# A cross network in Strassen form: the last unit's stores on other queues and in a new order, and two kinds of transposes at set times

## The chip, the cores and the metric

The kernel runs on one core of a Trainium2 chip. A core has TensorE (PE, matrix products), VectorE (DVE), ScalarE (ACT), GpSimd (POOL) and SyncE (SP), each with its own in-order queue of instructions, and DMA queues that SP, ACT and POOL fill and that share 16 DMA engines. The metric is the time of one execution on the device in microseconds; lower is better. Three executions of the kernel before took 2214.38, 2215.24 and 2218.46 us: the median is 2215.24 us.

## The reference

```python
x = x0                       # 16384 x 1024, bfloat16
for l in range(6):
    proj = x @ ws[l] + bs[l]     # ws[l]: 1024 x 1024
    x = x0 * proj + x
return x
```

Six layers, each a full matrix product of 16384 x 1024 by 1024 x 1024, followed by a product with the input x0 and the residual.

## The kernel before

**Work and tiles.** The 16384 rows are cut into 16 pairs of 1024 rows. A *unit* is one layer of one pair, so there are 96 units; two pairs form a group and take turns through the six layers (unit 2k is a layer of the even pair, unit 2k+1 the same layer of the odd pair), and the groups follow each other. Twelve units make a group; seven times in the program one group ends and the next begins. x is held transposed, as four quadrants of 512 features by 512 rows (`00`, `01`, `10`, `11`: feature half, row half).

**Products.** A unit does the 2x2 block product in Strassen-Winograd form with seven products P1 to P7 of 512 x 512 x 512 in place of eight. Each is four groups (`P1.0` to `P1.3`, by column block) of four matmuls 128x128 by 512 columns. Most units do three or four of the seven products with a second level of the same scheme (`5p1` to `5p7` and so on, groups of four matmuls with 256 columns). The sums of x's quadrants (T1 to T4) and the combination of the products (Q, U, V, W) are made on DVE; ACT takes results out of PSUM. The sums of weights are made once, in the first group, stored to DRAM (`Lc`) and reloaded for each later group into a ring of 12 buffers (`wp`).

**Order.** The program is written as named operations with engine, estimated duration and what they read and write. `schedule` (L69) makes from these a list by time, engine by engine: among those ready, the one with the earliest due time goes first; TensorE's order is given by hand in lists (`PE_FIRST` to `PE_LAST`, L17 to L44), one per kind of unit. `at=` gives an operation a time before which it isn't placed. These times only set the order in which instructions stand on each queue; on the chip an instruction runs when its queue reaches it and its semaphores are there. `plan_loads` (L146) puts the weight loads among them, and `pump` (L307) sends them on SP.

**SP's queue.** It carries the weight loads (L315), the loads of x0, which transpose from DRAM (`load`, L415; the DMA is L418), the transposes of finished results into row order (`tro`, L743; the DMA is L744) and their stores (`sto`, L751; L753), and most of the end's work. At a group boundary all four kinds meet: the next group's weights, the next odd pair's x0 (L436 to L438, loaded while unit l = 0 of the even pair runs), and the outputs of the finished even pair. There the lower two quadrants of x0 (`10` and `11`) are placed after `P4.0` of the unit two before:

```python
                load(pr, q, ARRIVE["next"] if u == 1 else 0.0, after=[f"ld11.{pr - 1}@{u - 4}"] + ([f"P4.0@{u - 2}"] if q[0] else []) if grp > 0 else ())
```

and the even pair's output transposes have no set time (L746).

**The last unit** (number 95, `last`) has only one level of products. Its four output quadrants leave by two ways. Q and the two halves U0 and U1 are put into x0's buffer by DVE, transposed by SP (`trQ`, `trU0`, `trU1`, L681) and stored by POOL's software queue (`stQ`, `stU0`, `stU1`, L684). V and W are transposed by TensorE (`tV.m`, `xW.m`, `tW.m`, L693, four of 128 columns each), copied out of PSUM by ACT and DVE (L703, L705) and stored in halves of 256 KB (`stVa`, `stVb`, `stWa` on SP, `stWb` on ACT, L712). While this goes on, the results of the other pair (number 14) leave by `tro` and `sto`.

Of the kernel before, what the change touches and what calls it, by code (L numbers as in the profile page):

```python
# [38 lines left out]
3p6 P7.0 4p2 3p3 4p6 3p7 P7.1 4p7 4p3 3p4 P7.3 P7.2 4p4  # L39
""".split()  # L40
PE_LAST = """
P1.0 P1.2 P1.3 P1.1 P2.0 P2.2 P2.1 P2.3 P6.0 P5.2 P5.1 P6.1 P5.0 P5.3 P3.1 P6.2 P3.0 P6.3 P3.2 P3.3 P7.0 P7.1 P7.3
P7.2 P4.0 P4.3 P4.2 tV.0 tV.1 xW.3 P4.1 xW.0 xW.2 tV.2 tV.3 xW.1 tW.0 tW.2 tW.3 tW.1
""".split()  # L44
ARRIVE = {"rows0": 4.9, "w0.1": 6.4, "rows1": 8.9, "rows2": 11.3, "w0.2": 11.9, "h0": 14.3, "h1": 15.5, "q": 17.5, "next": 21.0, "raw1": 40.0}

# [2 lines left out]
RING = 12  # L49
LOAD, BURST, LEAD, GRACE = 1.45, 2.9, 13, 4  # L50
STORED, SPARE = 12.0, 14.0
UNIT, LET = 22.68, 54.0
LOAD_ORDER = "1 5 2i 5i 4 2 3i 6 4i 3 7".split()
TURN = [
# [3 lines left out]
]  # L58


class Op:
# [130 lines left out]
def kernel(  # L192
# [7 lines left out]
    nc = tc.nc  # L200
# [4 lines left out]
    KH = KD // 2  # L205
# [5 lines left out]
    NGROUP = NPAIR // 2  # L211
# [136 lines left out]
    for u, (pr, l) in enumerate(units):  # L348
# [86 lines left out]

        if l == 0 and lane == 1:  # L436
            for q in QD:
                load(pr, q, ARRIVE["next"] if u == 1 else 0.0, after=[f"ld11.{pr - 1}@{u - 4}"] + ([f"P4.0@{u - 2}"] if q[0] else []) if grp > 0 else ())  # L438

        if grp == 0 and lane == 0:  # L440
            raw = lambda w, gl=gl: wt[(gl, w)]
# [188 lines left out]
        if not last:  # L630
            if not one:
                ttop("Q1", Q[:], Q[:], P1s[:], ADD, allm("Q") + allm("P1s"), allm("Q"))
            if not one:
                ttop("Ub", U[:], U[:], C3[:], ADD, allm("U") + allm("3c"), allm("U"))
            if "4" in inn:
                ttop("Wa", W[:], W[:], V[:], ADD, allm("W") + allm("V"), allm("W"))
            ttop("Ua", U[:], U[:], P5s[:], ADD, allm("U") + allm("5c"), allm("U"))
            ttop("Va", V[:], V[:], P5s[:], ADD, allm("V") + allm("5c"), allm("V"))
            for nm, C, q in (("Q", Q, (0, 0)), ("U", U, (0, 1)), ("V", V, (1, 1)), ("W", W, (1, 0))):
                if l == 0:  # L640
                    ttop(nm + "m", xblk(xst, *q), C[:], x0j(*q), MULT, allm(nm) + [X0[q]], [XO[q]] + ISW)
                    continue
                ttop(nm + "m", C[:], C[:], x0j(*q), MULT, allm(nm) + [X0[q]], allm(nm))
                if nm in DMA_RES.get(l, ""):
                    def acc(C=C, q=q, xst=xst):
                        nc.gpsimd.dma_start(xblk(xst, *q), C[:], accum_op=ADD)  # L646
                    op(f"{nm}x@{u}", "POOL", 1.0, ACCUM[(grp > 0) + (grp > 0 and l == L - 2 and lane)], acc, allm(nm) + [XO[q], "xbar"], [XO[q]])
                else:
                    ttop(nm + "x", xblk(xst, *q), C[:], xblk(xst, *q), ADD, allm(nm) + [XO[q]], [XO[q]])
        else:  # L650
            F0, F1 = (pr - 1) % 3, (pr - 2) % 3
            quad = lambda t: flat(t).rearrange("r (e n j k p) -> r e n j k p", e=2, n=2, j=KH, p=P)
            xfin, xo = quad(x0Ts[F0]), quad(xsts[F1])
            halves = lambda t: flat(t)[:, KH * NB:2 * KH * NB].rearrange("r (h j k p) -> r h j k p", h=2, j=KH, p=P)
            xfU, xoU = halves(x0Ts[F0]), halves(xsts[F1])
            XF = [f"x0.{F0}.{a}{b}" for a, b in QD]
            XT = [f"xs.{F1}.{a}{b}" for a, b in QD]
            r0 = pr * PR
            END = NU * 22.8
            half = lambda s, h: [f"{s}.{2 * h}", f"{s}.{2 * h + 1}"]  # L660
            ttop("Qm", Q[:], Q[:], x0j(0, 0), MULT, allm("Q") + [X0[0, 0]], allm("Q"))
            ttop("Qa", xfin[:, 0, 0], Q[:], xsj(0, 0), ADD,
                 allm("Q") + [XI[0, 0]] + XF, ["xfQ0", "xfQ1"])
            for h in range(2):
                sl = slice(h * KQ, (h + 1) * KQ)
                for nm, C, q in (("U", U, (0, 1)), ("V", V, (1, 1))):
                    ms = half(nm, h)
                    ttop(f"{nm}a{h}", C[:, :, sl], C[:, :, sl], P5s[:, :, sl], ADD, ms + half("5c", h), ms, n=1024)
                    ttop(f"{nm}m{h}", C[:, :, sl], C[:, :, sl], x0j(*q)[:, :, sl], MULT, ms + [X0[q]], ms, n=1024)
                ttop(f"Vx{h}", V[:, :, sl], V[:, :, sl], xsj(1, 1)[:, :, sl], ADD, half("V", h) + [XI[1, 1]], half("V", h), n=1024)  # L670
                ttop(f"Ux{h}", xfU[:, h], U[:, :, sl], xsj(0, 1)[:, :, sl], ADD, half("U", h) + [XI[0, 1]] + XF, [f"xfU{h}"], n=1024)
            for m in range(KH - 1):
                ttop(f"Wm{m}", mcol(W, m), mcol(W, m), mcol(x0j(1, 0), m), MULT, [f"W.{m}", X0[1, 0]], [f"W.{m}"], n=512)
            c = l * KD + 2 * KH - 1
            dve("Wm3", lambda c=c, x0T=x0T: nc.vector.scalar_tensor_tensor(
                out=mcol(W, KH - 1), in0=jr(pA[KH - 1]), scalar=b_all[:, c:c + 1], in1=mcol(x0j(1, 0), KH - 1), op0=ADD, op1=MULT),
                1024, [A[KH - 1], X0[1, 0]], [f"W.{KH - 1}"])
            outs = [("Q", xfin[:, 0, 0], xo[:, 0, 0], 0, 0, H)]
            outs += [(f"U{h}", xfU[:, h], xoU[:, h], NB, h * HQ, (h + 1) * HQ) for h in range(2)]
            for nm, src, dst, r, c0, c1 in outs:  # L680
                op("tr" + nm, "SP", 2.0, 6.0, lambda src=src, dst=dst: nc.sync.dma_start_transpose(  # L681
                    out=dst.rearrange("p j k r -> p (j k) r"), in_=src.rearrange("r j k p -> r (j k p)")),
                    (["xfQ0", "xfQ1"] if nm == "Q" else ["xf" + nm]) + XT, ["xo" + nm])
                op("st" + nm, "POOL", 1.0, 6.0, lambda dst=dst, r=r0 + r, c0=c0, c1=c1: nc.gpsimd.dma_start(  # L684
                    out[r:r + NB, c0:c1].rearrange("(j p) d -> p j d", p=P), dst.rearrange("p j k r -> p j (k r)")),
                    ["xo" + nm], ["out" + nm], due=END)
            for nm, C, bank, n in (("V", V, pX, 1), ("W", W, pA, 0)):
                for m in range(KH):
                    bn = (Xn if nm == "V" else A)[m]

                    def part(src, start, stop, bank=bank, m=m):
                        for j in range(KH):
                            nc.tensor.matmul(bank[m][:, j * P:(j + 1) * P], lhsT=src[:, j, m, :], rhs=ident[:],  # L693
                                             start=(start and j == 0), stop=stop, skip_group_check=True)
                    if nm == "W":
                        pe(f"xW.{m}", 0.25, lambda part=part, xsj=xsj: part(xsj(1, 0), True, False), [XI[1, 0]], [bn])
                    pe(f"t{nm}.{m}", 0.25, lambda part=part, C=C, nm=nm: part(C, nm == "V", True), [f"{nm}.{m}", bn], [bn])
                    on_act = nm == "V" or m in (0, 2)

                    def cp(bank=bank, m=m, n=n, on_act=on_act, xo=xo):  # L700
                        d, s_ = xo[:, 1, n][:, :, m, :], bank[m][:].rearrange("p (j r) -> p j r", r=P)
                        if on_act:
                            nc.scalar.copy(out=d, in_=s_)  # L703
                        else:
                            nc.vector.tensor_copy(out=d, in_=s_)  # L705
                    if on_act:
                        act(f"c{nm}.{m}", cp, [bn] + XT, [f"xo{nm}.{m}"])
                    else:
                        dve(f"c{nm}.{m}", cp, 1024, [bn] + XT, [f"xo{nm}.{m}"])

                def st2(k0, k1, eng=nc.sync, n=n, xo=xo, r0=r0):
                    eng.dma_start(out[r0 + n * NB:r0 + (n + 1) * NB, H + k0 * P:H + k1 * P].rearrange("(j p) d -> p j d", p=P),  # L712
                                  xo[:, 1, n][:, :, k0:k1].rearrange("p j k r -> p j (k r)"))
                op(f"st{nm}a", "SP", 1.0, 5.0, lambda st2=st2: st2(0, KQ), half(f"xo{nm}", 0), ["outa" + nm], due=END)
                op(f"st{nm}b", "SP" if nm == "V" else "ACT", 1.0, 5.0,
                   lambda st2=st2, nm=nm: st2(KQ, KH, nc.sync if nm == "V" else nc.scalar), half(f"xo{nm}", 1), ["outb" + nm], due=END)

        if grp == 0 and lane == 0:
            if first:
# [17 lines left out]
        for pt, qs in outs:  # L737
            sp = (pt // 2 * 2 + 1) % 3 if pt < NPAIR - 2 else (pt - 1) % 3
            for q in qs:
# [3 lines left out]
                def tro(q=q, pt=pt, fl=fl):  # L743
                    nc.sync.dma_start_transpose(out=fl.rearrange("p (f r) -> p f r", r=P),  # L744
                                                in_=xblk(xsts[pt % 3], *q).rearrange("p j k r -> p (j k r)"))
                op(f"tro{q[0]}{q[1]}.{pt}@{u}", "SP", 3.0, 8.0, tro, [f"xs.{pt % 3}.{q[0]}{q[1]}"], [sname],  # L746
                   after=[f"P7.0@{u}"] if pt % 2 else [])
                if pt % 2 and q == OUT[-1]:
                    fence(q, sp)

# [85 lines left out]
```

## Time and profile before

| | |
|---|---|
| median of three runs | 2215.24 us (2214.38 to 2218.46) |
| the profiled execution's own time | 2216.06 us |
| its span, first to last instruction | 2214.2 us |
| granted TensorE clock | 0.998 of full speed |
| instructions | 40542 |
| DMA | 512.30 MB, mean 231 GB/s |
| last matmul starts | 2202.36 us, ends 2202.75 |
| last output store is issued | 2204.34 us, on POOL |

The profile gives, for each engine, its busy time and instructions; for each group of equal instructions their mean duration; a list of waits (who waited for whom: us in total, times, longest); a time line (start and duration in us from the span's start, engine, source line, operation, and in brackets the idle time before it and what ended it); and DMA issues with the time to landing. A "q" behind an engine's name is its sequencer: `SPq` issues DMAs and is not counted as busy. A matmul's end is modelled, so the distance from one start to the next is the better measure. `L831` is the closing line: there SP waits for all landings, POOL drains, and a barrier of all engines ends the program.

### The profile page before, as it was taken

How to read it: one execution, taken by the hardware profiler on the slowest of the kernel's cores; microseconds unless marked ns; L12 is line 12 of the kernel's file. 1: busy time of each engine (PE TensorE's matmuls, PEld its weight loads, DVE VectorE, ACT ScalarE, POOL GpSimd, SP SyncE). 2: the span in 40 equal slices, each digit the busy share in tenths (PEclk: the TensorE clock that was granted, in tenths of full speed). 3: DMA queues.
4: the chain of work that ended last, by engine and by line, in shares of the span. 5: the costliest groups of instructions: out<-in, count | busy, mean ns of one | idle time of the engine just before them, and what ended most of it. 6: DMA issues, size and time to landing. Idle time of an engine off the chain costs nothing.

```text
span 2214.2 us, 40542 instructions
## 1 busy us (share of the span) xinstructions
PE 2198.7 (99%) x14925; PEld 1456.9 (66%) x14925; DVE 2150.6 (97%) x2583; ACT 2055.5 (93%) x3717; POOL 256.6 (12%) x327
## 2 busy tenths in 40 slices
PE   9999999999999999999999999999999999999997
PEld 5555566666666666666666666666666666666664
DVE  8999999999999999999999999999999999999996
ACT  7888899999999999999999999999999999999996
POOL 1122101111011110111001110011100111001110
PEclk9999999999999999999999999999999999999999
DMA  9698899988999889988999898998989979999896
GB/s 273 194 236 230 208 239 266 237 212 199 253 263 237 203 209 259 269 222 209 211 265 267 206 223 219 258 265 198 229 221 263 250 193 244 215 273 236 203 244 153
DMA packets 463528, 512.30 MB, mean 231 GB/s; under 512 B 270048, under 2 KB 382176, under 8 KB 463328
## 3 DMA queue, kind: packets, MB, share of 16 engines
q1 hardware_dynamic: 418352, 349.49, 55.6%
q0 software_dynamic: 44384, 159.94, 35.6%
q8 instruction: 117, 1.92, 0.3%
q14 instruction: 83, 0.68, 0.1%
q10 hardware_dynamic: 592, 0.27, 0.0%
HBM read 252.72 MB, written 58.20 MB: 140 GB/s over the span
## 4 chain that ended last, share of the span: by engine, by line
PE 98%; DMA 1%; SPq 0%; DVE 0%; ACT 0%; issue 0%; POOLq 0%; ACTq 0%; DVEq 0%
PE pA L394 49%; PE pX L588 47%; PE pX L394 2%; DMA xst<-x0T 0%; DMA x0T<-in_x_dram 0%; SPq L777 0%; ACT pX L403 0%; DVE ev L266 0%; SPq L784 0%; DVE T L266 0%; POOLq L831 0%; ACT ev L413 0%; DVE x0T L266 0%; SPq L790 0%; ACT ev L403 0%
## 5 line engine op out<-in xcount | busy, mean ns | idle before, releaser
L588 PEld LDWEIGHTS <-wp 128*128 128x128 bf16 x7464 | 730.0, 98 | 233.9 <-issue 3.2
L394 PE MATMUL pA<-T,wp 128*128 128x512 bf16 x3200 | 779.6, 380 | 0.0
L394 PEld LDWEIGHTS <-wp 128*128 128x128 bf16 x4768 | 466.2, 98 | 399.9 <-issue 2.3
L403 ACT CAST ev<-pX 128x512 bf16<-128x512 f32 x1144 | 649.3, 593 | 25.6 <-PE pX L588 21.1
L413 ACT ACTIVATE ev<-pA,b_all 128x512 bf16<-128x512 f32 x887 | 611.3, 693 | 38.9 <-PE pA L394 23.0
L588 PE MATMUL pX<-ti,wp 128*128 128x256 bf16 x4148 | 570.9, 273 | 0.0
L403 ACT COPY pX<-pX 128x512 f32<-128x512 f32 x678 | 388.6, 589 | 15.2 <-PE pX L588 11.2
L266 DVE TENSOR_TENSOR ev<-ev,ev 128x2048 bf16<-128x2048 bf16 (+1 forms) x282 | 341.8, 1219 | 12.7 <-ACT ev L413 5.3
L394 PE MATMUL pA<-xst,wp 128*128 128x512 bf16 x1056 | 260.6, 380 | 0.0
L413 ACT ACTIVATE xst<-pA,b_all 128x512 bf16<-128x512 f32 x324 | 222.2, 689 | 25.4 <-PE pA L394 15.7
L266 DVE TENSOR_TENSOR ev<-ev,x0T 128x2048 bf16<-128x2048 bf16 (+2 forms) x188 | 224.8, 1201 | 2.3 <-ACT ev L413 2.1
L588 PE MATMUL pX<-xst,wp 128*128 128x256 bf16 x1512 | 226.9, 273 | 0.0
L588 PE MATMUL pX<-T,wp 128*128 128x256 bf16 x1452 | 217.9, 273 | 1.3 <-ACT pX L403 1.2
L403 ACT CAST ip<-pX 128x512 bf16<-128x512 f32 x339 | 200.0, 591 | 6.8 <-DVE ev L266 3.8
L266 DVE TENSOR_TENSOR T<-xst 128x2048 bf16<-128x2048 bf16 x160 | 195.9, 1225 | 3.2 <-PE pA L394 2.4
L266 DVE TENSOR_TENSOR T<-xst,T 128x2048 bf16<-128x2048 bf16 x160 | 195.8, 1224 | 0.0
L266 DVE TENSOR_TENSOR ev<-ev,ip 128x1024 bf16<-128x1024 bf16 x284 | 194.9, 691 | 0.4 <-ACT ev L403 0.4
L646 POOL DMA_DIRECT2D xst<-ev x144 | 124.2, 865 | 581.2 <-ACT pX L403 151.1
L588 PEld LDWEIGHTS <-x0T 128*128 128x128 bf16 x1596 | 156.1, 98 | 48.0
L266 DVE TENSOR_TENSOR xst<-xst,ev 128x2048 bf16<-128x2048 bf16 x136 | 166.4, 1224 | 11.4 <-ACT xst L403 5.2
L266 DVE TENSOR_TENSOR xst<-xst,x0T 128x2048 bf16<-128x2048 bf16 x136 | 166.1, 1222 | 0.7
L646 POOL DMA_DIRECT2D xst<-xst x112 | 96.2, 859 | 508.5 <-ACT ev L413 151.9
(72 smaller groups left out, 1835.5 us busy)
## 6 DMA issues: line engine op xcount, KB each, us to landing
wp<-Lc SPq DMA_DIRECT2D x280, 512.0 KB, 5.4
xst<-ev POOLq DMA_DIRECT2D x144, 512.0 KB, 5.6
wp<-in_ws_dram SPq DMA_DIRECT2D x120, 512.0 KB, 5.6
xst<-xst POOLq DMA_DIRECT2D x112, 512.0 KB, 7.8
out_dram<-x0T SPq DMA_DIRECT2D x60, 512.0 KB, 5.2
x0T<-Lc SPq DMA_DIRECT2D x49, 512.0 KB, 5.2
x0T<-in_ws_dram SPq DMA_DIRECT2D x28, 512.0 KB, 6.5
Lc<-wp POOLq DMA_DIRECT2D x24, 512.0 KB, 5.2
```

The source lines that it names most:

```text
L266: nc.vector.tensor_tensor(out=o, in0=a, in1=b, op=op)
L394: newest["pe"] = nc.tensor.matmul(o, lhsT=wt[(gl, w)][:, k, m * P:(m + 1) * P], rhs=r, start=(start and k == 0), stop=(k == KH - 1), skip_ ...
L403: act(name, lambda: nc.scalar.copy(out=dst, in_=src), rd, wr)
L413: act(name, lambda: nc.scalar.activation(out=dst, in_=src, func=IDENT, bias=b_all[:, c:c + 1], scale=1.0), rd, wr, True)
L588: newest["pe"] = nc.tensor.matmul(o if kmajor else o.rearrange("p (j r) -> p j r", r=P), lhsT=wv[:, k, m * P:(m + 1) * P], rhs=rhs(k), sta ...
L646: nc.gpsimd.dma_start(xblk(xst, *q), C[:], accum_op=ADD)
```

## The change

Four things are changed.

- `PE_LAST`, the order of TensorE's groups in the last unit, is replaced. `P6` groups come earlier among `P1` and `P2`, halves are taken from the second down, and the transposes of W stand before the last of V.
- In the last unit a table `OUTQ` names the queue of each store: Q stays on POOL; U0, U1 and V0 go to SP; V1, W0 and W1 to ACT. Before, U0 and U1 were on POOL, V's halves and W's first half on SP, W's second half on ACT. (`V0` is the old `Va`, `V1` the old `Vb`, and the same for W.) The cost that the scheduler counts for a store on ACT goes from 1.0 to 0.45.
- x0's lower quadrants (`10`, `11`) for a group's odd pair are placed not before 22.68 u - 5.0 us, in place of after a TensorE group.
- The transposes of a finished even pair's output (`tro`, except in the last group) are placed not before 22.68 u + 46.0 us, u being the pair's last layer's unit plus one.

On the queues this gives: at each of the seven boundaries both lower loads of x0 stand before the output transposes of the even pair on SP (before, the first of the four transposes stood ahead of them). At the end SP sends pair 14's three transposes, `trQ`, three stores, `trU1`, `trU0`, `stU1`, `stV0`, `stU0`; POOL has `stQ` as its last DMA; ACT ends with `stV1`, `stW0`, `stW1`. On DVE and POOL the order of some operations of the last three units moves with it. No computation is added or left out.

```diff
 PE_LAST = """
-P1.0 P1.2 P1.3 P1.1 P2.0 P2.2 P2.1 P2.3 P6.0 P5.2 P5.1 P6.1 P5.0 P5.3 P3.1 P6.2 P3.0 P6.3 P3.2 P3.3 P7.0 P7.1 P7.3
-P7.2 P4.0 P4.3 P4.2 tV.0 tV.1 xW.3 P4.1 xW.0 xW.2 tV.2 tV.3 xW.1 tW.0 tW.2 tW.3 tW.1
+P1.1 P1.0 P6.1 P1.3 P1.2 P2.1 P2.0 P2.3 P6.2 P2.2 P5.3 P6.3 P5.2 P6.0 P5.1 P5.0 P3.3 P3.2 P3.1 P3.0 P7.0 P7.1 P7.3
+P7.2 P4.0 P4.3 P4.1 P4.2 tV.1 tV.0 xW.1 xW.3 xW.0 tW.1 xW.2 tW.3 tW.2 tV.3 tV.2 tW.0
 """.split()
...
-UNIT, LET = 22.68, 54.0
+UNIT, LET, LOWER, TURNS = 22.68, 54.0, 5.0, 46.0
...
+OUTQ = {"Q": "POOL", "U0": "SP", "U1": "SP", "V0": "SP", "V1": "ACT", "W0": "ACT", "W1": "ACT"}
...
-                load(pr, q, ARRIVE["next"] if u == 1 else 0.0, after=[f"ld11.{pr - 1}@{u - 4}"] + ([f"P4.0@{u - 2}"] if q[0] else []) if grp > 0 else ())
+                load(pr, q, ARRIVE["next"] if u == 1 else u * UNIT - LOWER if q[0] else 0.0, after=[f"ld11.{pr - 1}@{u - 4}"] if grp > 0 else ())
...
+            queue = {"SP": nc.sync, "ACT": nc.scalar, "POOL": nc.gpsimd}
...
-                op("st" + nm, "POOL", 1.0, 6.0, lambda dst=dst, r=r0 + r, c0=c0, c1=c1: nc.gpsimd.dma_start(
+                op("st" + nm, OUTQ[nm], 0.45 if OUTQ[nm] == "ACT" else 1.0, 6.0, lambda dst=dst, r=r0 + r, c0=c0, c1=c1, nm=nm: queue[OUTQ[nm]].dma_start(
...
-                op(f"st{nm}a", "SP", 1.0, 5.0, lambda st2=st2: st2(0, KQ), half(f"xo{nm}", 0), ["outa" + nm], due=END)
-                op(f"st{nm}b", "SP" if nm == "V" else "ACT", 1.0, 5.0,
-                   lambda st2=st2, nm=nm: st2(KQ, KH, nc.sync if nm == "V" else nc.scalar), half(f"xo{nm}", 1), ["outb" + nm], due=END)
+                for h in range(2):
+                    e = OUTQ[f"{nm}{h}"]
+                    op(f"st{nm}{h}", e, 0.45 if e == "ACT" else 1.0, 5.0, lambda st2=st2, h=h, e=e: st2(h * KQ, (h + 1) * KQ, queue[e]),
+                       half(f"xo{nm}", h), [f"out{h}{nm}"], due=END)
...
                 op(f"tro{q[0]}{q[1]}.{pt}@{u}", "SP", 3.0, 8.0, tro, [f"xs.{pt % 3}.{q[0]}{q[1]}"], [sname],
-                   after=[f"P7.0@{u}"] if pt % 2 else [])
+                   after=[f"P7.0@{u}"] if pt % 2 else [], at=u * UNIT + TURNS if not pt % 2 and grp + 1 < NGROUP else 0.0)
```

More of the change, by code (lines that the diff above doesn't have):

```diff
@@ L709, with st2 @@
                         dve(f"c{nm}.{m}", cp, 1024, [bn] + XT, [f"xo{nm}.{m}"])
-                def st2(k0, k1, eng=nc.sync, n=n, xo=xo, r0=r0):
+                def st2(k0, k1, eng, n=n, xo=xo, r0=r0):
                     eng.dma_start(out[r0 + n * NB:r0 + (n + 1) * NB, H + k0 * P:H + k1 * P].rearrange("(j p) d -> p j d", p=P),
                                   xo[:, 1, n][:, :, k0:k1].rearrange("p j k r -> p j (k r)"))
-                op(f"st{nm}a", "SP", 1.0, 5.0, lambda st2=st2: st2(0, KQ), half(f"xo{nm}", 0), ["outa" + nm], due=END)
-                op(f"st{nm}b", "SP" if nm == "V" else "ACT", 1.0, 5.0,
-                   lambda st2=st2, nm=nm: st2(KQ, KH, nc.sync if nm == "V" else nc.scalar), half(f"xo{nm}", 1), ["outb" + nm], due=END)
+                for h in range(2):
+                    e = OUTQ[f"{nm}{h}"]
+                    op(f"st{nm}{h}", e, 0.45 if e == "ACT" else 1.0, 5.0, lambda st2=st2, h=h, e=e: st2(h * KQ, (h + 1) * KQ, queue[e]),
+                       half(f"xo{nm}", h), [f"out{h}{nm}"], due=END)
         if grp == 0 and lane == 0:
```

## The prediction

> **What bounds the kernel now.** I read the page's busy shares first, then the waits by length, the time line round each wait that holds TensorE, and last the end of the program.
>
> ```profile
> PE 2198.7 (99%) x14925; PEld 1456.9 (66%) x14925; DVE 2150.6 (97%) x2583; ACT 2055.5 (93%) x3717; POOL 256.6 (12%) x327
> ```
> ```profile
> PE pX L588 <- ACT pX L403: 1.2, 3, 0.7
> ...
> DVE ti L266 <- DMA x0T<-in_x_dram: 3.8, 3, 2.0
> ```
> TensorE works through the whole span; DVE is nearly as full. Little is to be had: the few stalls of TensorE, and the end, when it has nothing left. The second fence is the list of waits (total us, times, longest). DVE waited three times for x0 transposed from DRAM, and I found these at 573, about 845 and 1663 us: each where a group of two row pairs begins and the SP queue is crowded. Round the longest, the time line shows (start, length):
>
> ```profile
> 560.76 4.88 SPq L744 DMA_TRANSPOSE x0T<-xst  x1
> 565.73 1.01 SPq L315 DMA_DIRECT2D wp<-Lc  x2
> 566.79 4.02 SPq L418 DMA_TRANSPOSE x0T<-in_x_dram  x1
> 570.91 0.53 SPq L315 DMA_DIRECT2D wp<-Lc  x1
> 571.49 4.36 SPq L418 DMA_TRANSPOSE x0T<-in_x_dram  x1
> ```
> ```profile
> 574.95 0.69 DVE L266 TENSOR_TENSOR ti<-x0T 128x1024 bf16<-128x1024 bf16 x1 [2.05 <-DMA x0T<-in_x_dram]
> ```
> ```profile
> 578.31 1.03 PE L394 MATMUL pA<-T,wp 128*128 128x512 bf16 x4
> 580.02 0.60 PE L588 MATMUL pX<-T,wp 128*128 128x256 bf16 x4 [0.69 <-ACT pX L403]
> ...
> 581.81 1.03 PE L394 MATMUL pA<-T,wp 128*128 128x512 bf16 x4
> ...
> 601.81 1.03 PE L394 MATMUL pA<-T,wp 128*128 128x512 bf16 x4
> 603.07 0.60 PE L588 MATMUL pX<-T,wp 128*128 128x256 bf16 x4 [0.24 <-ACT pX L403]
> ```
> An output transpose (L744) holds the SP queue for 4.88 us just ahead of the loads of x0's lower quadrants (L418). DVE starves 2.05 us, ACT waits for DVE, TensorE for ACT. A group of four 512-column matmuls is followed after 0.86 us when nothing waits (583.99 to 585.71 for two); here after 1.71 and 1.26 us, so 0.85 and 0.40 are lost, the second one unit later, when DVE is still behind. At 1668.82 and 1691.74 the same two places take 1.13 and 1.26 us: 0.27 and 0.40. Sum: 1.9 us. The other five boundaries show no such stall.
>
> The end, from the time line and from the instructions of the closing line (duration ns min/median/max, first to last start) and of the stores:
>
> ```profile
> 2202.35 1.09 ACT L703 CAST xst<-pA 128x512 bf16<-128x512 f32 x2
> 2203.47 0.42 ACTq L712 DMA_DIRECT2D out_dram<-xst  x1
> 2204.34 0.75 POOL L684 DMA_DIRECT2D out_dram<-xst  x1 [1.50 <-DMA xst<-x0T]
> ```
> ```profile
> L831 SPq EVENT_SEMAPHORE  x11: 17/28/28, 2209.3 to 2214.1; - x11
> L831 POOLq EVENT_SEMAPHORE  x4: 17/17/17, 2213.5 to 2214.1; - x4
> L831 POOLq DRAIN  x3: 46/99/9098, 2204.3 to 2213.9; - x3
> L831 SPq DRAIN  x3: 7/7/7, 2210.3 to 2213.7; - x3
> ```
> The last matmul ends at 2202.75. The last store is POOL's, issued at 2204.34; SP, which waits for every landing, is released at 2209.3 and reports at 2210.3. But POOL's own drain, begun at 2204.32 with that store still to issue, lasts 9.10 us, to 2213.42. The end barrier starts at 2213.46, 3.1 us after SP was ready, and takes 0.74 to 2214.2.
>
> **The change, part by part.** The order in which the two programs' instructions stand on each engine was compared; up to the last three units only SP's differs.
>
> *Group boundaries (seven).* SP now sends, in this order: one weight, the first lower quadrant of x0, two weights, the second lower quadrant, then the four output transposes and four stores. No instruction is added. At the boundary shown SP was free at 559.54 and waited for the transpose's data to 560.76; now the weight goes at once (its buffer's last matmuls, in TensorE's time line at 556.62, are over at 557.22), and the first lower load at about 560.1, 6.7 us before 566.79. That is over three times the 2.05 us that DVE waited, so I take the waits as gone, and with them 1.9 us of TensorE. Bounds: 0, if another wait takes their place; 1.9, all that is there. What is moved past: the two weights behind the first lower load gain the transpose's 4.88 and the 1.2 before it; one of them loses the load's 4.02, the other stood behind it already. The transpose itself goes back some 9 us, and its store with it; only output depends on it, and SP has nothing between 588.7 (584.58 + 4.13) and the weight at 594.17 to catch up in. Cost nothing; if that idle time were gone, the weight at 594.17 would come later by what is lacking.
>
> *Last unit, TensorE.* The same groups in another order, so the same time. One spot is tight: P6 of block column 1 follows its P1 after one other group. P1's evacuation copy ends 0.66 us after P1 (0.09 + 0.57, as 2176.78 to 2177.35 after P1.0's end at 2176.69), P6 would start 0.71 us after. I take 0; at most 0.1.
>
> *DVE and SP there.* POOL's four residual adds change order, so T1 and T2 of the last unit lie in the 2.36 us in which DVE waited ahead of T3 at 2172.84. From there, by 1.14 us an operation, Vx ends about 2181.5 (before 2183.75), Ux 2186.2 (2189.55), Qa 2188.6 (2187.16). Q's transpose goes out 1.5 us later, its store after it; but the three stores and transposes of the other pair go earlier, all ahead of U's transposes. U1 comes first now: ACT has evacuated its second P3 group by about 2192.3, and three DVE operations of 0.7 follow: 2194.5. U0's last P3 group stands where U1's stood (end 2193.1), so as U1 before at 2196.07, and one operation of V more lies between: 2197.05. U's transposes took 6.9 and 7.2 us to land, Q's 4.5: the later one lands between 2201.6 and 2204.3.
>
> *Stores.* U's halves go from POOL to SP, V's second and W's first from SP to ACT. On SP: U1, V0, U0, each 0.37 to 0.45 to issue; U0, last, at 2202 to 2204.4, which lands by 2209.3 at the 4.9 us of SP's slowest. On ACT four copies follow TensorE's fourth last group (end about 2202.0) at 0.47 each: 2204.1; then three stores at 0.42 and a little: 2204.1, 2204.55, 2205.0. Nothing waits behind them on ACT. The one ACT store of before landed 4.2 us after issue: the last lands at 2209.2, I take 2209.3. Bounds: 3.0 us, the quickest output store of the last stretch (L753), gives 2208.0; 5.2, the slowest (POOL's), 2210.2. I stay near 4.2, being the same queue and size and also sent into full DMA engines (their share was 0.95 to 1.02 from 2203.5 to 2207.5, and the bytes still to be written are the same). So the landing gains nothing.
>
> *POOL.* Its last DMA is now Q's store, at about 2193.5. The same 9.10 us drain from there ends near 2202.6, under TensorE's last matmuls. If the drain kept its 4.1 us behind the landing (2209.3 to 2213.4) instead, Q's store lands by 2199 and it ends by 2203. Covered either way, unless the drain waits for all stores (a rival). The end is then landing 2209.3 + 1.0 for SP's checks + 0.8 = 2211.1 in the old clock: 3.1 us less. With the landing's bounds 2.2 to 4.4.
>
> The page "VectorE: DVE Perf Modes" of the Trainium skill, section "The DRAIN you can't avoid", says that the drains at a program's end are a constant of some 12 ns on all five engines. By that rule POOL's drain costs nothing, the end hangs on the landing alone, and this part would be worth 0 in place of 3.1. The row of 9098 ns disagrees, and the sum goes by the row; what the rule gives is the first rival's time.
>
> **Sum.** 1.9 + 3.1 = 5.0 us from a profiled execution of 2216.06 (span 2214.2 and 1.9 round it): 2211.1. That execution lay 0.8 over the median 2215.24; taken off the median: 2210.2. Own range: 1.2 + 2.2 to 1.9 + 4.4, so 2208.9 to 2211.8. A measurement tells about 0.2%, 4.4 us, from no change; the forecast is only just past it.
>
> **Rivals.**
> 1. The drain hangs on every store, not on POOL's own: it then ends 4.1 us after the last landing whichever queue sent it, and the end stays. Only 1.9 is saved: 2213.3. For it: one drain of this length in the trace, so its cause isn't shown. Against: it began on POOL before SP's and ACT's stores had landed, with a POOL store in it.
> 2. The boundary stalls come back: DVE, 97% busy, meets another late operand, or the loads land no sooner since the DMA engines, not the queue, held them. Only 3.1 is saved: 2212.1. For it: one such load took 8.1 us to land. Against: boundaries with waits of 0 to 0.3 us show no stall at all.
> 3. Slower: weights late at every boundary. Two weights stand behind the first x0 load. The second was issued at 570.91, lands 5.4 us later (the page's median for weights), and its first group is the one at 578.31; I expect its issue at about 564.8. So it decides from an issue after 572.9, 8 us late. To end over 0.2% slower, 4.4 + 3.1 us over seven boundaries, 1.1 each, are wanted: an issue at 574.0 at each, and 2219.7. For it: SP is in order, and one buffer or load not yet ready holds all behind it. Against: what stands before that weight takes 6.1 us less than it did.
>
> **How the numbers follow.** Forecast 0.70; rival 1 0.09; rival 2 0.14; rival 3 0.07. Of the forecast's 0.70 about a fifth saves under 4.4 us. Faster: 0.56; within 0.2%: 0.14 + 0.23 = 0.37; slower 0.07. The range takes in rivals 1 and 2 and a little on both sides: 2208.7 to 2213.6.
>
> **What would show it.** DVE's waits for x0 from DRAM gone from the list and TensorE's 1.2 us with them; SP's first lower load before the L744 transpose; no POOL store after Q's, POOL's long drain ended before 2205; three stores on ACT's queue, the last landing near 2207.4 (2209.3 less 1.9), the span's end 1.8 us behind it. Wrong if the drain ends last again, if U's second half lands after 2205, or if a weight wait shows at the boundaries.

## The result, and the profile after

Eleven executions of each kernel on the same chip: the changed one took 2209.69 us (median; 2209.41 to 2210.59), the one before 2214.73 us (2213.33 to 2218.46). The ratio is 0.9976, with a 95% interval of 0.9966 to 0.9985: 5.04 us faster. The forecast was 2210.2 us.

The profiled execution of the changed kernel took 2209.69 us (span 2207.9); that of the kernel before had taken 2216.06 (span 2214.2), 1.3 over the median of its eleven. So the two profiles lie 6.3 us apart and the medians 5.0: what the profiles show in excess belongs to the execution, not to the change.

From the head of the page, and the four longest rows of TensorE's list of waits (engine, line waited at, what it waited for: us in total, times, longest):

```profile
PE 2197.0 (100%) x14925; PEld 1457.1 (66%) x14925; DVE 2149.4 (97%) x2583; ACT 2056.3 (93%) x3717; POOL 255.5 (12%) x325
```
```profile
PE pX L771 <- DVE ti L768: 1.2, 1, 1.2
PE pX L499 <- DVE x0T L503: 0.9, 1, 0.9
PE pX L395 <- ACT pX L404: 0.5, 1, 0.5
PE pX L395 <- DVE T L267: 0.4, 1, 0.4
```

The same instructions, but for two stores that POOL no longer sends, and the same bound. Lines in the changed kernel stand 1 to 3 lower down than before (L588 is now L589, L744 is L747, L831 is L834). The row of TensorE waiting at L589 for ACT, 1.2 us in three waits before, is gone, and DVE has no wait for x0 from DRAM left in its list.

SP's time line at the group boundary that the prediction showed (start, duration, engine, line, operation, transfers in a row):

```profile
558.90 3.65 SPq L316 DMA_DIRECT2D wp<-Lc  x3
562.64 4.64 SPq L419 DMA_TRANSPOSE x0T<-in_x_dram  x1
567.38 1.01 SPq L316 DMA_DIRECT2D wp<-Lc  x2
568.44 4.31 SPq L419 DMA_TRANSPOSE x0T<-in_x_dram  x1
572.84 5.77 SPq L747 DMA_TRANSPOSE x0T<-xst  x2
578.70 1.03 SPq L316 DMA_DIRECT2D wp<-in_ws_dram  x1
579.82 5.66 SPq L747 DMA_TRANSPOSE x0T<-xst  x2
585.58 4.05 SPq L756 DMA_DIRECT2D out_dram<-x0T  x4
```
```profile
573.05 0.68 DVE L267 TENSOR_TENSOR ti<-x0T 128x1024 bf16<-128x1024 bf16 x1
```
```profile
578.54 1.03 PE L395 MATMUL pA<-T,wp 128*128 128x512 bf16 x4
579.40 0.60 PE L589 MATMUL pX<-T,wp 128*128 128x256 bf16 x4
```

The loads of x0's lower quadrants go at 562.64 and 568.44, 4.15 and 3.05 us sooner than at 566.79 and 571.49, and all four output transposes (L747) stand behind them. DVE's operation on x0 starts with no idle time ahead of it (there is no bracket), and TensorE's next group follows 0.86 us after the group of 512 columns (578.54 to 579.40), the distance of an undisturbed one.

The end, from the time line and from the instructions of the closing line (duration ns min/median/max, first to last start):

```profile
2191.31 0.81 POOL L686 DMA_DIRECT2D out_dram<-xst  x1 [29.72 <-DMA xst<-x0T]
```
```profile
2201.28 2.30 ACTq L714 DMA_DIRECT2D out_dram<-xst  x3
```
```profile
L834 SPq EVENT_SEMAPHORE  x11: 17/28/28, 2202.0 to 2207.8; - x11
L834 POOLq DRAIN  x3: 46/99/10771, 2191.3 to 2207.6; - x3
L834 SPq DRAIN  x3: 7/7/7, 2207.0 to 2207.3; - x3
```

POOL's long drain is still there and has even grown, to 10.77 us, but it begins at 2191.29 and is over at 2202.06. ACT sends its three stores from 2201.28 on; the third lands last of all, at 2206.63 (the last semaphore update of a transfer in the trace). SP reports at 2207.08 (its second row of drains), and the span ends at 2207.85. From the last matmul's end (2200.32, before 2202.75) to the end of the span it now takes 7.53 us in place of 11.45.

### The profile page after: what moved, and what is told of

The parts are those of the page before. It is cut to its first block, busy times and chain, and to the rows that moved or that the text cites. A ratio compares the mean times of both kernels' runs of the same rounds, so it can differ in the third digit from the quotient of the medians.

```text
span 2207.9 us, 40540 instructions
## 1 busy us (share of the span) xinstructions
PE 2197.0 (100%) x14925; PEld 1457.1 (66%) x14925; DVE 2149.4 (97%) x2583; ACT 2056.3 (93%) x3717; POOL 255.5 (12%) x325
## 4 chain that ended last, share of the span: by engine, by line
PE 99%; SPq 0%; DMA 0%; ACT 0%; DVE 0%; issue 0%; DVEq 0%
PE pA L395 49%; PE pX L589 47%; PE pX L395 2%; DMA x0T<-in_x_dram 0%; SPq L780 0%; ACT xst L705 0%; PE pA L695 0%; SPq L787 0%; DVE T L267 0%; SPq L793 0%; SPq L790 0%; PE pX L695 0%; DVEq L267 0%
## 5 line engine op out<-in xcount | busy, mean ns | idle before, releaser
L589 PEld LDWEIGHTS <-wp 128*128 128x128 bf16 x7464 | 730.3, 98 | 231.0
L589 PE MATMUL pX<-ti,wp 128*128 128x256 bf16 x4148 | 570.8, 273 | 0.0
L589 PE MATMUL pX<-xst,wp 128*128 128x256 bf16 x1512 | 226.8, 273 | 0.0
L589 PE MATMUL pX<-T,wp 128*128 128x256 bf16 x1452 | 217.8, 273 | 0.0
L589 PEld LDWEIGHTS <-x0T 128*128 128x128 bf16 x1596 | 156.2, 98 | 47.9
```

Source lines behind the costliest of these rows:

```text
L589: newest["pe"] = nc.tensor.matmul(o if kmajor else o.rearrange("p (j r) -> p j r", r=P), lhsT=wv[:, k, m * P:(m + 1) * P], rhs=rhs(k), sta ...
```

## The experiments

Each edit is shown against the changed kernel; the values that it removes are those of the change. "Before" is the kernel before on the same chip: 2214.75 us for the first four kernels, 2214.83 for the next four, 2215.90 and 2215.93 for the last three. A median of one of these kernels is good to about 0.1%, 2 us, against that of before, but their own executions often lie within half a microsecond of each other; where these spreads don't overlap, kernels are compared with one another directly. The three groups of kernels ran on different chips, the last group on two, and the medians of the kernel before differ by up to 1.2 us between them; so a direct comparison across chips needs the traces beside it.

### Each half of the change alone

The boundary part alone: the last unit as before (queues, TensorE's order, estimated durations of the stores).

```diff
-OUTQ = {"Q": "POOL", "U0": "SP", "U1": "SP", "V0": "SP", "V1": "ACT", "W0": "ACT", "W1": "ACT"}
+OUTQ = {"Q": "POOL", "U0": "POOL", "U1": "POOL", "V0": "SP", "V1": "SP", "W0": "SP", "W1": "ACT"}
...
-P1.1 P1.0 P6.1 P1.3 P1.2 P2.1 P2.0 P2.3 P6.2 P2.2 P5.3 P6.3 P5.2 P6.0 P5.1 P5.0 P3.3 P3.2 P3.1 P3.0 P7.0 P7.1 P7.3
-P7.2 P4.0 P4.3 P4.1 P4.2 tV.1 tV.0 xW.1 xW.3 xW.0 tW.1 xW.2 tW.3 tW.2 tV.3 tV.2 tW.0
+P1.0 P1.2 P1.3 P1.1 P2.0 P2.2 P2.1 P2.3 P6.0 P5.2 P5.1 P6.1 P5.0 P5.3 P3.1 P6.2 P3.0 P6.3 P3.2 P3.3 P7.0 P7.1 P7.3
+P7.2 P4.0 P4.3 P4.2 tV.0 tV.1 xW.3 P4.1 xW.0 xW.2 tV.2 tV.3 xW.1 tW.0 tW.2 tW.3 tW.1
...
-   op("st" + nm, OUTQ[nm], 0.45 if OUTQ[nm] == "ACT" else 1.0, 6.0, ...
+   op("st" + nm, OUTQ[nm], 1.0, 6.0, ...
...
-   op(f"st{nm}{h}", e, 0.45 if e == "ACT" else 1.0, 5.0, ...
+   op(f"st{nm}{h}", e, 1.0, 5.0, ...
```

> The boundary part alone: the two set times for x0's lower loads and for the output transposes, with TensorE's order and the stores' queues of the last unit as before. Theory (the parts add: 1.9 us of TensorE's stalls at the boundaries, about 3.1 us of POOL's drain at the end): 1.9 us less than the kernel before, about 2212.8; DVE's wait for x0 from DRAM (3.8 us before) gone; from the last matmul to the end still 11.4 us, with POOL's drain over some 4 us after its own last store has landed. Rival (the whole gain is the end's, the boundary stalls are noise of one execution): within 0.5 us of the kernel before.

The last unit's part alone: the two set times taken out.

```diff
-   load(pr, q, ... else u * UNIT - LOWER if q[0] else 0.0, after=[f"ld11.{pr - 1}@{u - 4}"] if grp > 0 else ())
+   load(pr, q, ... else 0.0, after=[f"ld11.{pr - 1}@{u - 4}"] + ([f"P4.0@{u - 2}"] if q[0] else []) if grp > 0 else ())
-   after=[f"P7.0@{u}"] if pt % 2 else [], at=u * UNIT + TURNS if not pt % 2 and grp + 1 < NGROUP else 0.0)
+   after=[f"P7.0@{u}"] if pt % 2 else [])
```

> The last unit's part alone (stores' queues and TensorE's new order), with the boundaries as before. Theory: 3.1 us less than the kernel before and up to 3.9 as the changed kernel's profile has it (7.6 us from the last matmul to the end in place of 11.4): 2210.8 to 2211.6; DVE's waits for x0 from DRAM are back. Rival (boundary part is the gain): within 0.5 us of the kernel before.

Measured: boundary part alone 2213.48 us (2211.50 to 2214.36; ratio 0.9991, interval 0.9982 to 1.0), 1.27 less than before. Last unit's part alone 2210.95 us (2210.05 to 2214.16; ratio 0.9986, 0.9978 to 0.9995), 3.80 less. The two add to 5.07, the whole change gave 5.04: within the noise the parts add up. Each interval is wide, the first reaches no change at all, and a second pair that differs by the boundaries alone (further down: 2211.87 and 2209.82) gives 2.05 for the boundary part.

The traces agree on what each one does. With the boundary part alone, the closing line (same view and columns as above) is the old end, only sooner (11.46 us from the last matmul's end to the end of the span, 11.45 before):

```profile
L834 SPq EVENT_SEMAPHORE  x11: 17/28/28, 2207.1 to 2211.9; - x11
L834 POOLq EVENT_SEMAPHORE  x4: 17/17/17, 2211.2 to 2211.8; - x4
L834 POOLq DRAIN  x3: 46/99/9072, 2202.1 to 2211.7; - x3
L834 SPq DRAIN  x3: 7/7/7, 2207.7 to 2211.4; - x3
```

SP is ready at 2207.73, POOL's drain lasts to 2211.17. With the last unit's part alone, the waits at the boundaries are back, in the lists of TensorE and of DVE:

```profile
PE pX L589 <- ACT pX L404: 1.9, 4, 1.1
```
```profile
DVE ti L267 <- DMA x0T<-in_x_dram: 3.1, 2, 2.4
```

So the chain that the prediction read (x0 late, DVE waits, ACT, TensorE) comes with the old order on SP and goes with the new one. The size differs from execution to execution: in this profile, taken from an execution 2.5 us over its kernel's median, four distances lose 2.5 us (1.22 and 0.40 at one boundary, 0.47 and 0.40 at another), while the medians with and without it lie 1.3 us apart. It also adds to the spread: with the stores' queues as changed, 3.4 to 4.1 us from fastest to slowest with the old boundaries, 0.4 to 1.4 with the new ones. It isn't alone in that: with the new boundaries, but one of POOL's stores landing last, the spread is still 2.7 to 2.9 us (this section's first run and the one with U0 on POOL).

### Which of the two set times

```diff
-   load(pr, q, ... else u * UNIT - LOWER if q[0] else 0.0, after=[f"ld11.{pr - 1}@{u - 4}"] if grp > 0 else ())
+   load(pr, q, ... else 0.0, after=[f"ld11.{pr - 1}@{u - 4}"] + ([f"P4.0@{u - 2}"] if q[0] else []) if grp > 0 else ())
```

> The changed kernel without the set time of x0's lower loads (they are placed after the TensorE group again); the set time of the output transposes stays, so these still stand behind the lower loads on SP, and the loads come one weight earlier still. Theory (what counts is that no output transpose stands ahead of the lower loads): as the changed kernel, 2209.7 within 0.4 us, no DVE wait for x0 from DRAM. Rival (the loads' own set time matters): 1 to 1.9 us slower, with those waits back.

Measured: 2209.52 us (2209.35 to 2209.92), the same as the whole change. What counts is that the output transposes are held back. The other half, the set time for the loads alone, wasn't run: in the program's order the first transpose then still stands ahead of the lower loads, as before.

### Is it the drain that sets the end?

U0's store, the last that SP sends, goes back to POOL's queue; all else as changed.

```diff
-OUTQ = {"Q": "POOL", "U0": "SP", "U1": "SP", ...
+OUTQ = {"Q": "POOL", "U0": "POOL", "U1": "SP", ...
```

> The changed kernel with one store, U's first half, put back on POOL's queue; all else as changed. Theory (POOL's drain ends about 4.05 us after POOL's own last store has landed: 2213.42 against 2209.31 before, 2202.06 against 2198.04 after): that store lands near 2206.5 in the profile, the drain ends near 2210.5, and the execution is 2.5 to 3.2 us longer than the changed kernel, 2212.2 to 2212.9. Rival (the end hangs on the last landing of any queue): within 0.5 us of 2209.7.

Measured: 2213.07 us (2210.66 to 2213.36; ratio 0.9990, 0.9980 to 0.9999), 3.4 more than with all of the change. Its closing line:

```profile
L834 POOLq DRAIN  x3: 46/108/8530, 2202.0 to 2211.1; - x3
L834 SPq DRAIN  x3: 7/7/7, 2207.4 to 2210.8; - x3
```

One store of 256 KB on another queue brings the wait back: SP is ready at 2207.49, POOL at 2210.57. The last landing of any queue did not move against the changed kernel (2206.51 and 2206.63), so the 3.1 us from 2207.49 to 2210.57 are the drain's alone.

The drain's length is not a constant. The trace gives, for each kernel, when POOL's own last transfer landed and when the long drain ended (us):

```
kernel                          drain from   to        length   POOL's last landing   end - landing   last landing of all
before                          2204.32      2213.42    9.10    2209.31               4.10            2209.31
boundary part alone             2202.10      2211.17    9.07    2207.07               4.10            2207.07
U0 on POOL                      2202.03      2210.57    8.53    2206.51               4.06            2206.51
changed                         2191.29      2202.06   10.77    2198.04               4.02            2206.63
last unit's part alone          2194.70      2205.28   10.58    2201.26               4.02            2209.95
Q on SP (no POOL store there)   2160.57      2169.59    9.02    2165.62               3.97            2205.35
```

It ends 3.97 to 4.10 us after the landing of the last transfer that POOL itself sent, however long it has stood and whatever is still under way on the other queues; in the seven profiles not listed the distance is 3.97 to 4.02. That is the second of the two readings for which the prediction had found the drain covered, and it throws out both a fixed 9.1 us and a drain that hangs on every store.

### The queues without the new order

TensorE's order and the boundaries as before, OUTQ as changed.

```diff
-P1.1 P1.0 P6.1 P1.3 ...
+P1.0 P1.2 P1.3 P1.1 ...
...
-   load(pr, q, ... else u * UNIT - LOWER if q[0] else 0.0, ...
+   load(pr, q, ... else 0.0, after=[f"ld11.{pr - 1}@{u - 4}"] + ([f"P4.0@{u - 2}"] if q[0] else []) if grp > 0 else ())
...
-   after=[f"P7.0@{u}"] if pt % 2 else [], at=u * UNIT + TURNS if not pt % 2 and grp + 1 < NGROUP else 0.0)
+   after=[f"P7.0@{u}"] if pt % 2 else [])
```

> Only the stores' queues are new; TensorE's order of the last unit and the boundaries are as before. Theory (the end's gain is the drain's, not TensorE's order): within 0.7 us of the run with the whole last unit's part, 2210.8 to 2212. Rival (the new order of TensorE's groups carries it, by bringing the other pair's stores ahead of U's transposes): over 1 us slower than that run, 2212.5 or more.

Measured: 2211.87 us (2210.16 to 2213.60; ratio 0.9988, 0.9979 to 0.9997). That is 0.92 more than the last unit's part alone, inside the spread of either, a spread that comes at least in part from the old boundaries. So the test was made again without them: the changed kernel with only the old TensorE order (the two lines of each in full above).

```diff
-P1.1 P1.0 P6.1 P1.3 ...
-P7.2 P4.0 P4.3 P4.1 ...
+P1.0 P1.2 P1.3 P1.1 ...
+P7.2 P4.0 P4.3 P4.2 ...
```

> The changed kernel with TensorE's old order of groups in the last unit; queues and boundaries as changed. Theory as predicted (the order is worth nothing by itself, the drain is all): 2209.7 within 0.4 us. Rival, from the difference of the two runs before (2211.87 with the queues alone, 2210.95 with the new order too): 0.9 us slower than the changed kernel, 2210.6, with U's second half landing later against the last matmul.

Measured: 2209.82 us (2209.42 to 2210.78) against 2209.69. As the change stands, the new order is worth about 0.1 us, less than can be told apart.

### What sets the last landing?

First, one store fewer on ACT's queue, where three follow each other at the very end.

```diff
-... "V1": "ACT", "W0": "ACT", "W1": "ACT"}
+... "V1": "ACT", "W0": "SP", "W1": "ACT"}
```

> The changed kernel with W's first half stored by SP in place of ACT, so that ACT sends two stores and SP four. In the changed kernel's profile ACT's third store takes 1.20 us to issue and lands last, at 2206.63, while SP issues nothing after 2201.92. If the landing hangs on ACT's issues: about 0.5 us faster, 2209.2. If on the DMA engines, which are full from 2202 to 2206: the same within 0.2 us.

Measured: 2209.71 us (2209.53 to 2210.12), last landing 2206.58 against 2206.63. The issue on ACT does not set it.

Then, Q's store off POOL's queue, so that POOL sends nothing in the last unit.

```diff
-OUTQ = {"Q": "POOL", ...
+OUTQ = {"Q": "SP", ...
```

> The changed kernel with Q's store on SP too, so that POOL sends no DMA after its residual adds of the unit before. Theory (POOL's drain ends about 4.05 us after POOL's own last landing, and in the changed kernel that is at 2202, under TensorE's last matmuls): POOL's drain ends before 2180, no time gained, 2209.7 within 0.4 us; slower by up to 0.5 if SP, in order, sends U's transposes later for it. Rival (POOL's drain costs something wherever it lies): over 0.5 us faster.

Measured: 2208.65 us (2208.28 to 2208.69; ratio 0.9968, 0.9956 to 0.9981): a miss for the theory, and 1.04 us faster than the changed kernel, with no overlap of the spreads. (On this same chip the runs with the held-back transposes alone and with W0's store on SP, which time like the changed kernel, took 2209.52 and 2209.71.) By the number it is the rival's time, but the drain can't be the reason, since it was covered in both (over at 2202.06 and at 2169.59); the next run, in which POOL sends nothing either, bears this out. The last landing came sooner: 2205.35 in place of 2206.63. Here is the last stretch of each kernel in steps of 2 us (the step; then busy us of PE, PEld, DVE, ACT and POOL; the granted clock; the mean busy share of the 16 DMA engines; GB/s). The changed kernel:

```profile
2192.00:2194.00 2.00, 2.00 (x11) 0.88 (x9) 1.97 (x5) 1.65 (x3) 0.12 (x1) 1.00 1.01 315
2194.00:2196.00 2.00, 2.00 (x11) 0.91 (x10) 2.00 (x5) 1.42 (x3) 0.00 (x0) 1.00 1.08 359
2196.00:2198.00 2.00, 2.00 (x18) 1.18 (x17) 2.00 (x5) 1.01 (x2) 0.00 (x0) 1.00 1.14 127
2198.00:2200.00 2.00, 2.00 (x40) 2.00 (x38) 2.00 (x6) 1.64 (x4) 0.00 (x0) 1.00 0.91 186
2200.00:2202.00 2.00, 0.32 (x6) 0.15 (x3) 0.54 (x1) 1.74 (x4) 0.00 (x0) 1.00 0.72 207
```

With Q's store on SP:

```profile
2192.00:2194.00 2.00, 2.00 (x11) 0.92 (x10) 1.97 (x4) 1.55 (x3) 0.00 (x0) 1.00 1.02 323
2194.00:2196.00 2.00, 2.00 (x11) 0.88 (x9) 2.00 (x4) 1.37 (x2) 0.00 (x0) 1.00 1.17 219
2196.00:2198.00 2.00, 2.00 (x19) 1.25 (x18) 2.00 (x5) 1.15 (x2) 0.00 (x0) 1.00 1.10 311
2198.00:2200.00 2.00, 2.00 (x40) 2.00 (x36) 2.00 (x5) 1.64 (x4) 0.00 (x0) 1.00 0.99 234
2200.00:2202.00 2.00, 0.18 (x4) 0.00 (x1) 0.41 (x1) 1.60 (x4) 0.00 (x0) 1.00 0.91 254
```

Rate times 2 us, added up, gives the bytes moved from 2192 to 2202: 2388 KB in the changed kernel, 2682 KB here. The 294 KB are 1.0 us at the 286 and 289 GB/s of the changed kernel's steps from 2202 to 2206. And SP's time line of the two, first the changed kernel, then Q's store on SP:

```profile
2192.22 6.28 SPq L683 DMA_TRANSPOSE xst<-x0T  x2
2199.16 0.37 SPq L686 DMA_DIRECT2D out_dram<-xst  x1
```
```profile
2192.07 2.27 SPq L683 DMA_TRANSPOSE xst<-x0T  x1
2194.39 1.02 SPq L686 DMA_DIRECT2D out_dram<-xst  x1
2195.47 1.76 SPq L683 DMA_TRANSPOSE xst<-x0T  x1
2197.28 1.06 SPq L686 DMA_DIRECT2D out_dram<-xst  x1
```

In the changed kernel POOL's packets and those of U's first transpose share the engines; that transpose lands at 2199.14, only then can U1's store be sent (2199.16), and from 2199.5 to 2200.0 the engines move next to nothing (1 KB by the packets in the trace). With Q's store between the two transposes in SP's own queue, the first one lands at 2197.03 and U1's store goes at 2197.28. Is it POOL's queue that does this, or any second queue? Q's store on ACT tells:

```diff
-OUTQ = {"Q": "POOL", ...
+OUTQ = {"Q": "ACT", ...
```

> The changed kernel with Q's store on ACT's queue; POOL again sends no DMA in the last unit, and SP's order is the changed kernel's. Theory: it is POOL's queue, whose packets shared the 16 engines badly with U's transposes, that cost 1.0 us; then it ends as with Q's store on SP, 2208.65, within 0.4, with the last landing near 2205.4 and U's transposes landed sooner than 2199.1 and 2201.5. Rival: any store sent beside the transposes from another queue costs this, and the gain was SP's sending one thing after the other; then 2209.7, within 0.4, with the last landing near 2206.6.

Measured: 2209.68 us (2209.36 to 2209.82), the rival's time. ACT sent it at 2192.43; U's first transpose again landed at 2199.12, and the engines again had nothing to do behind it:

```profile
2198.00:2200.00 2.00, 2.00 (x40) 2.00 (x37) 2.00 (x5) 1.64 (x4) 0.00 (x0) 1.00 0.76 149
```

So POOL's queue is not to blame, and POOL's drain, which is as early here as with Q's store on SP, isn't either. The same store on ACT, but some 5 us later, tests the other half of the story, that what is lost is the early landing of the first transpose:

```diff
-    ["xo" + nm], ["out" + nm], due=END)
+    ["xo" + nm], ["out" + nm], due=END, at=END + 8 if nm == "Q" else 0.0)
...
-OUTQ = {"Q": "POOL", ...
+OUTQ = {"Q": "ACT", ...
```

> Q's store on ACT's queue as in the run before, but held back in the plan to behind ACT's last evacuation copy of W, so some 5 us later, about 2197.6: U's first transpose then has the 16 engines to itself, the second one shares them with Q's store. Theory: what costs 1 us is that Q's store, sent from a second queue while the first of U's transposes runs, makes that transpose land only with the second, at 2199.1, so that U1's store isn't there to fill the engines, which stand empty at 2199.5. Then here the first transpose lands by 2196.7, U1's store is issued before 2198, no such gap, and 2208.7 is reached within 0.4. Rival: any store from another queue beside any of U's transposes costs as much, 2209.7 within 0.4; or it is later still, since 512 KB go last.

Measured: 2209.38 us (2208.98 to 2209.59): 0.3 us below the run before by the medians, with spreads that overlap. The theory's time was missed, and the time lies in the rival's range. Of what the theory said of the trace, U1's store did go early (first transpose landed at 2196.95, where by 2196.7 was expected; store sent at 2196.96), but the gap did not vanish. The step in question shows it.

```profile
2196.00:2198.00 2.00, 2.00 (x20) 1.27 (x19) 2.00 (x5) 1.17 (x2) 0.00 (x0) 1.00 0.81 153
```

The gap is only moved. Now both transposes are through by 2197.98, the two stores have only just been sent (2196.96 and 2197.58), and between 2197.5 and 2197.75 no packet begins in the trace. The rival's reason isn't shown either, since Q's store hardly stood beside a transpose here. An early landing of the first transpose was not enough by itself; the engines ran dry behind it.

The last kernel asks how much of the change the better place of Q's store needs: TensorE's old order and no set time for the x0 loads.

```diff
-OUTQ = {"Q": "POOL", ...
+OUTQ = {"Q": "SP", ...
...
-P1.1 P1.0 P6.1 P1.3 ...
+P1.0 P1.2 P1.3 P1.1 ...
...
-   load(pr, q, ... else u * UNIT - LOWER if q[0] else 0.0, ...
+   load(pr, q, ... else 0.0, ...
```

> Q's store on SP's queue, and of the change only the other queues and the set time of the output transposes; TensorE's order in the last unit and the x0 loads' own due time as before the change. Theory: by the single runs the order is worth 0.1 us and the loads' time nothing, and Q's place on SP 1.0, so 2208.7, within 0.4. Rival: SP's order with Q's store depends on TensorE's order, U0 and U1 come in the other turn, and the 1.0 us is not there: 2209.8.

Measured: 2209.61 us (2209.23 to 2209.69), the rival's time: the gain is gone. Its SP queue shows what is different:

```profile
2188.23 3.34 SPq L747 DMA_TRANSPOSE x0T<-xst  x1
2191.66 0.53 SPq L756 DMA_DIRECT2D out_dram<-x0T  x1
2192.29 1.73 SPq L683 DMA_TRANSPOSE xst<-x0T  x1
```

With the old order, the last output transpose and two stores of the other pair still stand among those of the last unit (in the changed kernel they are all sent ahead of U's transposes). The engines are full all the time here (share 1.06 to 1.16 from 2192 to 2202), they just have more left. For the five kernels, from the windows (rate times 2 us):

```
kernel                    KB moved after 2192   of these by 2202   left at 2202   last landing   last matmul to last landing   time, us
changed                   3556                  2388               1168           2206.63        6.31                          2209.69
Q on ACT                  3510                  2384               1126           2206.35        6.16                          2209.68
Q on SP, old order        3880                  2792               1088           2206.65        6.13                          2209.61
Q on ACT, later           3500                  2546                954           2205.99        5.83                          2209.38
Q on SP                   3510                  2682                828           2205.35        5.17                          2208.65
```

What is left at 2202, when ACT's last stores are being sent, orders the stretch from the last matmul's end to the last landing in all five profiles. The first three times can't be told apart. The middle three ran on other chips than Q's store on SP, and against the kernel before on its own chip each of the last four has a ratio of 0.9968 to 0.9971, which tells nothing apart. What speaks for comparing them directly is that the last matmul ends at 2200.16 to 2200.52 in all five profiles: up to there the work took the same time on each chip. By that comparison TensorE's order is worth about 1 us with Q's store on SP (2209.61 against 2208.65), and 0.1 us with the gap on the DMA engines. The loads' set time, also taken out there, cost nothing in its own run, and SP sends the last unit's transfers in the same order with and without it. Q's store on SP, with all of the rest of the change, is the fastest version found: 2208.65 us.

## Why the prediction was right, and where it was off

The forecast's sum stood on two terms, and both were there, each by the mechanism named.

- **Boundaries, 1.9 us.** Right in the chain; its size stays open. The 1.9 was added up from four places of one execution that was 1.3 us over the median of eleven. For that execution it was too small: subtracting the starts of TensorE's instructions in the two profiles, one by one, the kernel before falls behind by 1.59 us between 515 and 646 us and by 1.01 between 1554 and 1815, 2.6 in all. What the prediction did not count are groups behind the four places that start 0.05 to 0.08 us late each. In medians the part is worth 1.27 alone, 1.26 between the last unit's part alone and the whole change, and 2.05 with TensorE's old order (2211.87 and 2209.82). Taking 0.8 off the sum at the end allowed for the slow execution in the level of the forecast; the term kept the size of that one profile.
- **What is moved past.** No weight came late. The first lower load went at 562.64 rather than at about 560.1, behind weight loads that held SP until 562.55; 4.15 us sooner instead of 6.7 was still enough to remove a wait of 2.05. That the transposes could go back at no cost held, and it is they alone that had to be moved.
- **Last unit, TensorE: nothing.** Held; there was no stall at P6 of block column 1, and the old order costs 0.1 us, too little to tell. With Q's store on SP the order counts, as the last runs showed, through what it does to SP's queue.
- **Stores.** ACT's three went at 2201.28, 2201.80 and 2202.39; moved by the 2.43 us by which TensorE ended sooner, 2203.71 to 2204.82 in the old clock, for a forecast of 2204.1 to 2205.0. The last landed 4.24 us after its issue (forecast 4.2), and SP's last, U0's, well ahead of it, at 2204.76. The bound of 5.2 us, taken as the slowest, left out a store of the other pair on SP (issued at 2193.92 in the kernel before) that took 6.07; nothing came of it. "The landing gains nothing" was near: 2209.06 in the old clock, 2209.3 forecast. That the time to landing came out so well is luck in part: with Q's store on SP the same last store landed 3.11 us after its issue.
- **The end, 3.1 us.** Right in the mechanism, and by the traces too small: 3.80 in medians with TensorE's new order, 2.88 with the old one. In the profiles the stretch behind the last matmul shrank by 3.92 us, and by 3.3 and 3.7 in the two with the queues changed and the old order; of the 0.8 by which 3.92 is above the forecast, 0.55 are SP's checks behind the last landing, 0.45 us where I had kept the 1.0 of before, and 0.24 the landing.
- **The drain.** The prediction kept open whether it lasts 9.1 us or ends 4.1 us behind POOL's landing. It is the second, in every profile. Rival 1, a drain that hangs on every store, fell with the profile of the changed kernel: drain over at 2202.06, last landing 2206.63. The rule of the Trainium skill (page "VectorE: DVE Perf Modes", section "The DRAIN you can't avoid"), a constant of some 12 ns on all five engines, is stated for the drains that the runtime puts round a kernel, in preamble and postamble. The drains here stand at the kernel's own closing line and don't follow it: 8.5 to 10.8 us on POOL, worth 3.4 us where a store of POOL's is the last. The prediction set that rule against this row; no row of these traces shows the drains of which the page speaks.
- **Rivals 2 and 3.** Neither happened: no operand came late in place of the old one, and the boundaries show no wait for a weight.

The saving forecast was 5.0 us and 5.04 were measured, closer than either term was known: by the medians of the two halves one is 0.6 too large and the other 0.7 too small. That they cancel is luck. What was missing altogether is what the later runs found: that the last landing goes with how much the DMA engines have moved by the time of the last issue, so that it was in reach of the change to move it. That rests on five profiles; why a store from another queue holds a transpose up is not shown. I had taken the share near 1 behind 2203.5 and concluded that nothing could be gained; the loss lay earlier, in a stretch whose steps show 127 and 186 GB/s at shares of 1.14 and 0.91.

## What to carry to other kernels

- Look at the end of the program for the engine that reports last, not only for the last landing. Here the last transfer that POOL sent held its drain for 4 us after landing; let POOL's last transfer land 4 us before the others, or send it from elsewhere.
- Of the transfers on one in-order queue, hold back those that only output waits for, ahead of the loads that the next stage waits for. It needed one due time.
- When the last stretch is bound by DMA, count the bytes still to move at the time of the last issue, and look for the step where the engines move few. A busy share near 1 does not say that they move much: shares of 1.14 and 1.08 went with 127 and 359 GB/s.

## What was not expected of the hardware

- POOL's drain at the end follows POOL's own last landing by 3.97 to 4.10 us; the drains of SP take 7 ns.
- A store on a second queue, POOL's or ACT's, beside a transpose from SBUF holds that transpose up: issued at 2192.1 to 2192.2, it landed at 2199.1 in both cases, and at 2196.95 to 2197.03 where Q's store stood behind it in SP's own queue or went some 5 us later. Over all profiles it takes 6.8 to 7.0 us to land in the ten kernels with Q's store beside it from POOL or ACT, and 4.0 to 5.0 in the other three. Sent one after the other from one queue, the same two transfers were both through at 2198.43.
- The third of ACT's stores in a row took 1.20 us to issue (the first 0.41, the second 0.49), and 0.50 in the kernel with Q's store on SP. Why is open; it delayed nothing, as the run with W0's store on SP shows.
